# Cosine attention followed by a gated feed-forward on one core: the last batch's layout and stores, one kv copy, two x chunks placed anew, six x buffers

## The chip, the cores and the metric

The kernel runs on one core of a Trainium2 chip. Its time is in device microseconds, from start to end of one execution; a profile of one execution gives a span that is about 1.8 us shorter. Engines are called PE (matrix engine; PEld is its weight load), DVE (VectorE), ACT (ScalarE), POOL (GpSimd) and SP (SyncE). A DMA transfer lands when the trace shows its completion; a stop is a stretch in which PE has nothing to do. A run counts as slow when it lies over 1.5% above the fastest of its kernel.

Ratios are the mean time of one kernel's fast runs over that of the kernel before in the same rounds, so not quite the ratio of the medians quoted beside them. Stops of PE are worked out from start times as in the prediction.

## The reference

Shortened; what is left out is reshaping and types.

```python
def _attn_ref(q, k, v):                     # (8, 8, 576, 64): batch, head, position, dim
    theta = pi / 2 * arange(S) / S          # cos, sin of it: one weight per position
    phi = lambda x: concat([relu(x) * cos, relu(x) * sin], -1)
    kv  = einsum('bhsf,bhsd->bhfd', phi(k), v);  z = sum(phi(k), axis=2)
    num = einsum('bhsf,bhfd->bhsd', phi(q), kv)
    den = einsum('bhsf,bhf->bhs', phi(q), z)[..., None] + 1e-06
    return num / den

def reference(...):
    x = attn_out.transpose(0, 2, 1, 3).reshape(4608, 512)
    return ((x @ w1) * (x @ w2) @ w3) @ w_out        # 512 -> 1024 -> 1024 -> 512
```

## The kernel before

Tokens go through the feed-forward in nine tiles of 512. The attention of batch t+1 is woven between the matmuls of tile t: each tile has 24 slots, and a schedule hangs small pieces of attention into them. A batch of 576 positions is five chunks (four of 128 rows, one of 64). Per chunk: features of k, q and v; kv accumulated over the chunks; num (the product with q's features); division into a block xblk; transposition of that block into xT, the operand of the feed-forward. For batches 0 and 1 PE transposes and an engine copies the result; from batch 2 on a DMA transposes.

```python
        if i == NCH - 1:                                    # kv of batches 1 to 7 complete
            kvs = sm.tile([P, H, D + 1], BF16, name="kvs", bufs=2)
            nc.scalar.copy(out=kvs[:, 0:4, :], in_=kvt[:, 0, 0:260])
            nc.vector.tensor_copy(out=kvs[:, 4:8, :], in_=kvt[:, 1, 0:260])
...
        xblk = sm.tile([P, 2, 4, D], BF16, name="xblk", bufs=4)      # in num(b, c)
        def normalize():
            den = sm.tile([P, 2, 4], FP32, name="den")
            nc.vector.tensor_scalar_add(out=den[rows], in0=n4[:, :, :, 64], scalar1=1e-6)
            nc.vector.reciprocal(out=den[rows], in_=den[rows])
            nc.vector.tensor_tensor(out=xblk[rows], in0=n4[:, :, :, 0:D], in1=..., op=ALU.mult)
...
        if b >= 2:                                                   # in x_tr(b, c)
            nc.sync.dma_start_transpose(out=xT[t][:, :, ds(o, R)], in_=xf)
            return
...
        for kc in range(4):
            nc.tensor.transpose(pst[:, kc, 0:R], xf[:, ts(kc, 128)], identb[rows, rows])
        copy = nc.vector.tensor_copy if by_vector else nc.scalar.copy
        copy(out=xT[t][:, :, ds(o, R)], in_=pst[:, 0:4, 0:R])
...
        for i, rows in enumerate(parts):                    # store: two halves of 64 partitions
            on = eng[i % 2] if isinstance(eng, tuple) else eng
            on.dma_start(out=rows[:, :, cols], in_=osb[64 * i:64 * i + rows.shape[0], :, cols])
...
        if t == NT - 1:                                     # the last 128 rows of the output
            for half in range(2):
                cols, n = ts(half, 256), 256
                ops = ffn_tile()
                ...                                         # eight matmuls of n columns
                nc.vector.tensor_copy(out=osb[:, 1, cols], in_=ops[:, 0:n])
                store((nc.sync, nc.scalar), osb[:, 1:2, :], 4 * t + 3, 1, cols)
```

In batches 1 to 7 positions are laid on partitions as 64 x 5 and 64 x 4, so an output tile of 128 partitions falls into two separate blocks of rows, and each store into two halves. Batch 0 alone is laid out as 128 x 4 rows plus 64.

Of the kernel before, what the change touches and what calls it, by code (L numbers as in the profile page):

```python
# [16 lines left out]
P = 128  # L17
H, S, D = 8, 576, 64
F = 2 * D
NCH = 5  # L20
# [48 lines left out]
def kernel(  # L69
# [34 lines left out]



    raw = {}

    def load(b, which, part=None):
        for name in which:  # L110
            src = {"k": k, "v": v, "q": q}[name]
            if part != 1:
                raw[b, name] = ld.tile([P, H, NCH, D], BF16, name=name + "s")
                nc.gpsimd.dma_start(
                    out=raw[b, name][0:64, :, :, :].rearrange("p h j d -> p h (j d)"),
                    in_=src[b, :, 0:320, :].rearrange("h (p j) d -> p h (j d)", j=5))
            if part != 0:
                nc.gpsimd.dma_start(
                    out=raw[b, name][64:128, :, 0:4, :].rearrange("p h j d -> p h (j d)"),
                    in_=src[b, :, 320:S, :].rearrange("h (p j) d -> p h (j d)", j=4))  # L120

    def load_first(eng, t, src, c0=0, n=4):
        rows = src[0, :, 0:512, :].rearrange("h (p j) d -> p h j d", j=4)
        eng.dma_start(out=t[:, :, c0:c0 + n, :].rearrange("p h j d -> p h (j d)"),  # L124
                      in_=rows[:, :, c0:c0 + n, :].rearrange("p h j d -> p h (j d)"))

    def load_first4(eng, t, src):
        eng.dma_start(out=t[0:64, :, 4, :], in_=src[0, :, 512:S, :].rearrange("h p d -> p h d"))

    woutb = wst.tile([P, 8, DM], BF16, name="woutb", bufs=1)  # L130
    w3b = wst.tile([P, 8, DFF], BF16, name="w3b", bufs=1)
# [118 lines left out]
    def features(b, dst, src, c, cos=True, sin=True, scalar_heads=H):  # L250

        R = ROWS[c]
        at = c if b == 0 else NCH + c
        if cos:
            nc.vector.tensor_scalar(out=dst[:R, c, :, 0:D], in0=src[:R, :, c, :], scalar1=0.0,  # L255
                                    scalar2=cosv[:R, at:at + 1], op0=ALU.max, op1=ALU.mult)
        if sin:
            n = scalar_heads
            nc.scalar.activation(out=dst[:R, c, 0:n, D:F], in_=src[:R, 0:n, c, :], func=ACTF.Relu,  # L259
                                 scale=sinv[:R, at:at + 1], bias=0.0)  # L260
            if n < H:
                nc.vector.tensor_scalar(out=dst[:R, c, n:H, D:F], in0=src[:R, n:H, c, :],
                                        scalar1=0.0, scalar2=sinv[:R, at:at + 1],
                                        op0=ALU.max, op1=ALU.mult)
# [16 lines left out]
    def kv_chunk(b, c, i):  # L281
        kp, qp, va = feat[b]
        if i == 0:
            att_of(b)["kv"] = ps_att.tile([P, 2, 512], FP32, name="pnum")
        kvt = att[b]["kv"]
        for h in range(H):
            nc.tensor.matmul(kvt[:, h // 4, ds((h % 4) * 65, 65)], lhsT=kp[:, c, h, :],  # L287
                             rhs=va[:, c, h, 0:D + 1], start=(i == 0 and h % 4 == 0),
                             stop=(i == NCH - 1 and h % 4 == 3))
        if i == NCH - 1:  # L290
            kvs = sm.tile([P, H, D + 1], BF16, name="kvs", bufs=2)
            nc.scalar.copy(out=kvs[:, 0:4, :], in_=kvt[:, 0, 0:260])
            nc.vector.tensor_copy(out=kvs[:, 4:8, :], in_=kvt[:, 1, 0:260])  # L293
            att[b]["kvs"] = kvs

    def kv_first():
# [38 lines left out]
    def num(b, c, chain=True):  # L335
        rows = out_rows(b, c)
        R = ROWS[c]
        at = columns_of(b, c) - rows.start
        qpT, kvs = att[b]["qpT"], att[b]["kvs"]
        if b == 0 and c == 0:  # L340
            nt = ps_first.tile([P, 2, 512], FP32, name="pfirst")
        else:
            nt = ps_att.tile([P, 2, 512], FP32, name="pnum")
        for h in range(H):
            nc.tensor.matmul(nt[:, h // 4, ds((h % 4) * 65, 65)], lhsT=qpT[:, h, ds(at, 128)],  # L345
                             rhs=kvs[:, h, :], start=True, stop=True)
        n4 = nt[rows, :, 0:260].rearrange("p g (h e) -> p g h e", e=65)
        xblk = sm.tile([P, 2, 4, D], BF16, name="xblk", bufs=4)
        att[b]["x"][c] = xblk

        def normalize():
# [3 lines that stand above are left out]
            nc.vector.tensor_tensor(out=xblk[rows], in0=n4[:, :, :, 0:D],  # L355
                                    in1=den[rows].unsqueeze(3).to_broadcast([R, 2, 4, D]),
                                    op=ALU.mult)

        if chain:
            normalize()  # L360
        return normalize
# [24 lines left out]
    def attention_at(b, slots, kv, tr, nu, xt):  # L386

        each = list(enumerate(order_of(b)))
        for i, c in each:
            slots[kv[i]].append(lambda c=c, i=i: kv_chunk(b, c, i))  # L390
            if c not in dma_q(b):
                slots[tr[i]].append(lambda c=c: q_tr(b, c))
        for i, c in each:
            if xt[i] > nu[i]:
                slots[xt[i]].append(lambda c=c: x_tr(b, c))
        for i, c in each:
            slots[nu[i]].append(lambda c=c: num(b, c))
            if xt[i] == nu[i]:
                slots[xt[i]].append(lambda c=c: x_tr(b, c))


    def rows_of(b, c, n):

        if b == 0:
            if c == 4:
                return [out[512:S, :].rearrange("(p j) m -> p j m", j=1)]
            return [out[0:512, :].rearrange("(p j) m -> p j m", j=4)[:, c:c + n, :]]
        lower = out[ds(b * S, 320), :].rearrange("(p j) m -> p j m", j=5)
        upper = out[ds(b * S + 320, 256), :].rearrange("(p j) m -> p j m", j=4)
        return [h[:, c:c + n, :] for h in ((lower,) if c == 4 else (lower, upper))]  # L410

    def store(eng, osb, g, n, cols=slice(0, DM)):

        pair, r = divmod(g, 9)
        b, c = (2 * pair, r) if r < 4 else (2 * pair + 1, r - 5)
        if r == 4:
            parts = rows_of(2 * pair, 4, 1) + rows_of(2 * pair + 1, 4, 1)
        elif n == 1 or c + n <= 4:
            parts = rows_of(b, c, n)
        else:  # L420
            parts = None
        if parts is None or (r == 4 and n > 1):
            for i in range(n):
                store(eng, osb[:, i:i + 1, :], g + i, 1, cols)
            return
        for i, rows in enumerate(parts):
            on = eng[i % 2] if isinstance(eng, tuple) else eng
            on.dma_start(out=rows[:, :, cols], in_=osb[64 * i:64 * i + rows.shape[0], :, cols])  # L428

    ffn_tiles = [0]  # L430

# [16 lines left out]
    def ffn_groups(t):  # L448
# [8 lines left out]
        def on_half(half):  # L457

            for pair in range(2):
                a, b = ffn_tile(), ffn_tile()  # L460
                if pair == 0:
                    for quarter in range(2):
                        for i in range(2):
                            for ps, w in ((a, w1b), (b, w2b)):
                                products(ps[:, ds(256 * i + 128 * quarter, 128)], w, i,
                                         ds(256 * half + 128 * quarter, 128))
                            if half == 0 and quarter == 0 and i == 0:
                                yield
                        if quarter == 0:
                            yield  # L470
                else:
                    for ps, w in ((a, w1b), (b, w2b)):
# [24 lines left out]
        for ms in range(3 if t == NT - 1 else 4):  # L497
# [6 lines left out]
            if ms % 2 == 0:  # L504
                if 1 <= t <= 4:
                    osb = held_pool[0].tile([P, 2, 512], FP32, name="held")
                else:
                    osb = fsb.tile([P, 2, 512], FP32, name="osb", bufs=2)
            nc.scalar.copy(out=osb[:, ms % 2, :], in_=ops[:, :])  # L509
            if t == NT - 1:  # L510
                store((nc.sync, nc.scalar), osb[:, ms % 2:ms % 2 + 1, :], 4 * t + ms, 1)
            elif ms % 2 == 1 and 1 <= t <= 4:
                held.append((osb, 4 * t + ms - 1))
            elif ms % 2 == 1:
                store(nc.gpsimd, osb[:, :, :], 4 * t + ms - 1, 2)
            yield
        if t == NT - 1:
            for half in range(2):
                cols, n = ts(half, 256), 256
                ops = ffn_tile()  # L520
                for jc in range(8):
                    nc.tensor.matmul(ops[:, 0:n], lhsT=abT[:, jc, ts(3, 128)],  # L522
                                     rhs=w34b[:, jc, cols], start=(jc == 0), stop=(jc == 7))
                nc.vector.tensor_copy(out=osb[:, 1, cols], in_=ops[:, 0:n])
                store((nc.sync, nc.scalar), osb[:, 1:2, :], 4 * t + 3, 1, cols)
            yield


# [58 lines left out]
    for t in range(NT):  # L587
        slots = [[] for _ in range(24)]
        if t == 0:
            slots[1].append(lambda: x_tr(0, 1, by_vector=True))  # L590
            slots[1].append(lambda: q_tr(0, 3, evac=False)[1]())
            slots[1].append(lambda: num(0, 2))
            slots[3].append(lambda: x_tr(0, 2))
            slots[3].append(lambda: num(0, 3))
            slots[4].append(lambda: x_tr(0, 3))
            slots[6].append(lambda: prep_q(0, 4))
            slots[11].append(lambda: feature_buffers(1))
            slots[8].append(lambda: q_tr(0, 4))
# [72 lines left out]
```

## Time and profile before

| | kernel before |
|---|---|
| median of 3 runs | 252.97 us (252.49 to 253.37) |
| the profiled run | 253.31 us, span 251.5 us, clock 1.0 |
| PE / DVE / ACT / POOL busy | 97% / 55% / 50% / 36% |
| DMA engines' busy slices, first 100 us | nearly all 9 tenths |
| landing of an x transpose after its issue | 2.3 us at least, 5.0 median, 8.6 at most |

PE is the bound; what counts is where it stands still. The views that show this are in the prediction.

### The profile page before, as it was taken

To read this page: it belongs to the slowest core of one execution; us is meant where nothing else is said; L and a number is where in the kernel's file an instruction comes from. 1 tells how busy PE (TensorE), PEld (TensorE's weight loads), DVE (VectorE), ACT (ScalarE), POOL (GpSimd) and SP (SyncE) were. 2 spreads that over 40 slices of the span, in tenths; PEclk is the share of its full clock that TensorE was granted. 3 is DMA by queue.
4 is the path that set the end of the run, shared out by engine and by line. 5 is a ranking of instruction groups with operands and counts; after the bars stand their busy time and mean duration, and the time that the engine had idled before them with its cause. 6 is when DMAs were issued, how large, how long until landed. Compare 5 with 4: busy or idle time off the path is not lost.

```text
span 251.5 us, 4960 instructions
## 1 busy us (share of the span) xinstructions
PE 243.8 (97%) x1871; PEld 129.9 (52%) x1871; DVE 137.2 (55%) x336; ACT 126.8 (50%) x217; POOL 90.4 (36%) x171
## 2 busy tenths in 40 slices
PE   8899999999999999999999999999999999999993
PEld 2578555666555455545544554555455444444442
DVE  7675665747789628904971594279128504303321
ACT  2676316925976656565655665565532242323320
POOL 7764155540524612441442327270464040022000
PEclk9999999999999999999999999999999999999999
DMA  7999999999989999999899999997699842014014
GB/s 197 180 194 199 210 204 204 198 199 198 254 112 176 182 184 139 213 152 154 127 135 153 179 127 138 242 236 151 120 275 272 113 122 59 3 39 128 0 46 126
DMA packets 79161, 39.86 MB, mean 159 GB/s; under 512 B 46752, under 2 KB 75680, under 8 KB 79136
## 3 DMA queue, kind: packets, MB, share of 16 engines
q0 software_dynamic: 35488, 27.20, 67.5%
q1 hardware_dynamic: 43248, 11.80, 34.4%
q10 hardware_dynamic: 400, 0.52, 0.6%
q8 instruction: 15, 0.25, 0.4%
q14 instruction: 10, 0.08, 0.1%
HBM read 38.80 MB, written 9.44 MB: 192 GB/s over the span
## 4 chain that ended last, share of the span: by engine, by line
PE 86%; DMA 7%; DVE 2%; ACT 2%; issue 1%; POOL 1%; POOLq 0%; DVEq 0%
PE ffnps L454 47%; PE ffnps L500 22%; PE ffnps L222 5%; PE pnum L345 3%; PE pnum L287 3%; DMA xT<-xblk 3%; DMA qs<-in_q_dram 3%; PE pst L318 2%; PE pst L210 1%; PE pst L382 1%; ACT kp L259 1%; PE ffnps L522 1%; DVE xblk L355 1%; POOL vs L124 0%; DVE abT L495 0%
## 5 line engine op out<-in xcount | busy, mean ns | idle before, releaser
L495 DVE TENSOR_TENSOR abT<-asb,ffnps 128x512 bf16<-128x512 bf16 x68 | 46.3, 681 | 71.3 <-PE ffnps L454 69.9
L454 PE MATMUL ffnps<-xT,w1b 128*128 128x512 bf16 (+2 forms) x320 | 74.9, 357 | 0.3 <-DVE xT L384 0.2
L454 PE MATMUL ffnps<-xT,w2b 128*128 128x512 bf16 (+2 forms) x320 | 74.9, 357 | 0.0
L491 ACT CAST asb<-ffnps 128x512 bf16<-128x512 f32 x68 | 39.8, 586 | 59.9 <-PE ffnps L454 50.1
L500 PE MATMUL ffnps<-w34b,abT 128*128 128x512 bf16 x280 | 63.2, 379 | 0.6 <-DVE abT L495 0.6
L454 PEld LDWEIGHTS <-w1b 128*128 128x128 bf16 x320 | 29.4, 98 | 29.5 <-issue 0.7
L500 PEld LDWEIGHTS <-abT 128*128 128x128 bf16 x280 | 26.8, 98 | 32.0 <-DVE abT L495 1.0
L454 PEld LDWEIGHTS <-w2b 128*128 128x128 bf16 x320 | 26.8, 98 | 20.3
L259 ACT ACTIVATE qp<-qs,sinv 128x512 bf16<-128x512 bf16 (+2 forms) x40 | 28.3, 718 | 1.7 <-DMA qs<-in_q_dram 1.6
L428 POOL DMA_DIRECT2D out_dram<-osb x20 | 10.6, 535 | 51.0 <-ACT osb L509 51.0
L355 DVE TENSOR_TENSOR xblk<-pnum,den 128x512 bf16<-128x512 f32 (+1 forms) x39 | 26.9, 690 | 2.5 <-DMA xT<-xblk 1.1
L279 POOL COPY va<-vs 128x512 bf16<-128x512 bf16 (+1 forms) x30 | 18.5, 625 | 22.9 <-DMA vs<-in_v_dram 22.9
L259 ACT ACTIVATE kp<-ks,sinv 128x512 bf16<-128x512 bf16 (+1 forms) x35 | 24.9, 723 | 0.0
L509 ACT COPY osb<-ffnps 128x512 f32<-128x512 f32 x19 | 11.1, 586 | 22.7 <-PE ffnps L500 22.7
L345 PEld LDWEIGHTS <-qpT 128*128 128x128 bf16 x320 | 15.1, 98 | 8.8 <-issue 0.8
L345 PE MATMUL pnum<-kvs,qpT 128*128 128x65 bf16 x312 | 16.5, 194 | 0.3 <-DVE kvs L293 0.3
L287 PEld LDWEIGHTS <-kp 128*128 128x128 bf16 x280 | 13.1, 98 | 7.1
L255 DVE TENSOR_SCALAR qp<-qs,cosv 128x512 bf16<-128x512 bf16 (+1 forms) x40 | 16.4, 416 | 0.5 <-DMA qs<-in_q_dram 0.5
L509 ACT COPY held<-ffnps 128x512 f32<-128x512 f32 x16 | 9.4, 586 | 14.3 <-PE ffnps L500 14.3
L222 PE MATMUL ffnps<-woutb,w3T 128*128 128x512 bf16 x64 | 15.4, 379 | 0.0
L535 POOL COPY seen<-kp 128x1 bf16<-128x1 bf16 (+1 forms) x20 | 3.8, 188 | 29.2 <-DVE kp L255 20.5
L287 PE MATMUL pnum<-va,kp 128*128 128x65 bf16 x280 | 14.1, 193 | 0.0
(87 smaller groups left out, 194.6 us busy)
## 6 DMA issues: line engine op xcount, KB each, us to landing
out_dram<-held POOLq DMA_DIRECT2D x10, 256.0 KB, 4.7
qs<-in_q_dram POOLq DMA_DIRECT2D x9, 256.0 KB, 8.1
ks<-in_k_dram POOLq DMA_DIRECT2D x7, 320.0 KB, 10.3
qs<-in_q_dram POOLq DMA_DIRECT2D x7, 320.0 KB, 7.4
vs<-in_v_dram POOLq DMA_DIRECT2D x7, 320.0 KB, 8.7
w3b<-in_moe_w_dram POOLq DMA_DIRECT2D x8, 256.0 KB, 12.7
ks<-in_k_dram POOLq DMA_DIRECT2D x7, 256.0 KB, 5.6
vs<-in_v_dram POOLq DMA_DIRECT2D x7, 256.0 KB, 9.8
```

Source lines behind the costliest of these rows:

```text
L222: nc.tensor.matmul(acc[:, :], lhsT=w3T[:, lc, :], rhs=woutb[:, lc, :], start=(lc == 0), stop=(lc == 7))
L255: nc.vector.tensor_scalar(out=dst[:R, c, :, 0:D], in0=src[:R, :, c, :], scalar1=0.0, scalar2=cosv[:R, at:at + 1], op0=ALU.max, op1=ALU.mult)
L259: nc.scalar.activation(out=dst[:R, c, 0:n, D:F], in_=src[:R, 0:n, c, :], func=ACTF.Relu, scale=sinv[:R, at:at + 1], bias=0.0)
L279: eng.tensor_copy(out=feat_of(b)[2][:R, c, :, 0:D], in_=raw[b, "v"][:R, :, c, :])
L287: nc.tensor.matmul(kvt[:, h // 4, ds((h % 4) * 65, 65)], lhsT=kp[:, c, h, :], rhs=va[:, c, h, 0:D + 1], start=(i == 0 and h % 4 == 0), sto ...
L345: nc.tensor.matmul(nt[:, h // 4, ds((h % 4) * 65, 65)], lhsT=qpT[:, h, ds(at, 128)], rhs=kvs[:, h, :], start=True, stop=True)
L355: nc.vector.tensor_tensor(out=xblk[rows], in0=n4[:, :, :, 0:D], in1=den[rows].unsqueeze(3).to_broadcast([R, 2, 4, D]), op=ALU.mult)
L454: nc.tensor.matmul(out, lhsT=w[:, kc, ts(jc, 128)], rhs=x[:, kc, tok], start=(kc == 0), stop=(kc == 3))
L491: nc.scalar.copy(out=asb[:], in_=aT[:, :])
L495: nc.vector.tensor_mul(out=abT[:, jc, :], in0=asb[:], in1=bT[:, :])
L500: nc.tensor.matmul(ops[:, :], lhsT=abT[:, jc, ts(ms, 128)], rhs=w34b[:, jc, :], start=(jc == 0), stop=(jc == 7))
L509: nc.scalar.copy(out=osb[:, ms % 2, :], in_=ops[:, :])
```

## The change

Its intent: close the short stops of PE, and shorten the end. The last batch gets batch 0's layout so that the last tile is stored in whole tiles of 128 partitions; kv is copied by one instruction; in the first tile the fourth num comes ahead of the third chunk's transposes, and the fourth chunk's transposes move behind the first matmuls of the second half; batch 1's fourth chunk is copied by VectorE; the last 128 rows of the output are finished in pieces of 256, 128 and 128 columns in place of two of 256, each stored by one queue; there are six x buffers, and one output buffer moves to another pool to make room.

```diff
+    own = (0, B - 1)                       # batches laid out as 128 x 4 rows + 64
...                                         (loads, tables and output rows follow `own`)
-            nc.scalar.copy(out=kvs[:, 0:4, :], in_=kvt[:, 0, 0:260])
-            nc.vector.tensor_copy(out=kvs[:, 4:8, :], in_=kvt[:, 1, 0:260])
+            nc.vector.tensor_copy(out=kvs[:].rearrange("p (g h) e -> p g (h e)", g=2),
+                                  in_=kvt[:, :, 0:260])
...
-        xblk = sm.tile([P, 2, 4, D], BF16, name="xblk", bufs=4)
+        xblk = sm.tile([P, 2, 4, D], BF16, name="xblk", bufs=6)
...
-                slots[xt[i]].append(lambda c=c: x_tr(b, c))
+                slots[xt[i]].append(lambda c=c, i=i: x_tr(b, c, by_vector=(i == 3)))
...
-                            if half == 0 and quarter == 0 and i == 0:
+                            if quarter == 0 and i == 0:
                                 yield
-                        if quarter == 0:
+                        if half == 0 and quarter == 0:
                             yield
...
-                    osb = fsb.tile([P, 2, 512], FP32, name="osb", bufs=2)
+                    pool = (fsb, held_pool[0])[ms // 2]
+                    osb = pool.tile([P, 2, 512], FP32, name="osb", bufs=1)
...
-                store((nc.sync, nc.scalar), osb[:, ms % 2:ms % 2 + 1, :], 4 * t + ms, 1)
+                store((nc.sync, nc.scalar)[ms % 2], osb[:, ms % 2:ms % 2 + 1, :], 4 * t + ms, 1)
...
-            for half in range(2):
-                cols, n = ts(half, 256), 256
+            for at, n, eng in ((0, 256, nc.scalar), (256, 128, nc.sync), (384, 128, nc.scalar)):
+                cols = ds(at, n)
...
-                store((nc.sync, nc.scalar), osb[:, 1:2, :], 4 * t + 3, 1, cols)
+                store(eng, osb[:, 1:2, :], 4 * t + 3, 1, cols)
...
-            slots[3].append(lambda: x_tr(0, 2))
             slots[3].append(lambda: num(0, 3))
-            slots[4].append(lambda: x_tr(0, 3))
+            slots[3].append(lambda: x_tr(0, 2))
+            slots[5].append(lambda: x_tr(0, 3))
```

More of the change, by code (lines that the diff above doesn't have):

```diff
@@ L102, with load_first, load_first4 @@
     ctx.enter_context(tc.manual_schedule())
+    own = (0, B - 1)
     raw = {}
+    def load_first(eng, t, src, c0=0, n=4, b=0):
+        rows = src[b, :, 0:512, :].rearrange("h (p j) d -> p h j d", j=4)
+        eng.dma_start(out=t[:, :, c0:c0 + n, :].rearrange("p h j d -> p h (j d)"),
+                      in_=rows[:, :, c0:c0 + n, :].rearrange("p h j d -> p h (j d)"))
+    def load_first4(eng, t, src, b=0):
+        eng.dma_start(out=t[0:64, :, 4, :], in_=src[b, :, 512:S, :].rearrange("h p d -> p h d"))
     def load(b, which, part=None):
@@ L113, in load @@
                 raw[b, name] = ld.tile([P, H, NCH, D], BF16, name=name + "s")
+            if b in own:
+                if part != 1:
+                    load_first(nc.gpsimd, raw[b, name], src, b=b)
+                if part != 0:
+                    load_first4(nc.gpsimd, raw[b, name], src, b=b)
+                continue
+            if part != 1:
                 nc.gpsimd.dma_start(
@@ L120, in load @@
                     in_=src[b, :, 320:S, :].rearrange("h (p j) d -> p h (j d)", j=4))
-    def load_first(eng, t, src, c0=0, n=4):
-        rows = src[0, :, 0:512, :].rearrange("h (p j) d -> p h j d", j=4)
-        eng.dma_start(out=t[:, :, c0:c0 + n, :].rearrange("p h j d -> p h (j d)"),
-                      in_=rows[:, :, c0:c0 + n, :].rearrange("p h j d -> p h (j d)"))
-    def load_first4(eng, t, src):
-        eng.dma_start(out=t[0:64, :, 4, :], in_=src[0, :, 512:S, :].rearrange("h p d -> p h d"))
     woutb = wst.tile([P, 8, DM], BF16, name="woutb", bufs=1)
@@ L252, in features @@
         R = ROWS[c]
-        at = c if b == 0 else NCH + c
+        at = c if b in own else NCH + c
         if cos:
@@ L402, in rows_of @@
     def rows_of(b, c, n):
-        if b == 0:
+        if b in own:
             if c == 4:
-                return [out[512:S, :].rearrange("(p j) m -> p j m", j=1)]
-            return [out[0:512, :].rearrange("(p j) m -> p j m", j=4)[:, c:c + n, :]]
+                return [out[b * S + 512:(b + 1) * S, :].rearrange("(p j) m -> p j m", j=1)]
+            rows = out[b * S:b * S + 512, :].rearrange("(p j) m -> p j m", j=4)
+            return [rows[:, c:c + n, :]]
         lower = out[ds(b * S, 320), :].rearrange("(p j) m -> p j m", j=5)
@@ L426, in store @@
         for i, rows in enumerate(parts):
-            on = eng[i % 2] if isinstance(eng, tuple) else eng
-            on.dma_start(out=rows[:, :, cols], in_=osb[64 * i:64 * i + rows.shape[0], :, cols])
+            eng.dma_start(out=rows[:, :, cols], in_=osb[64 * i:64 * i + rows.shape[0], :, cols])
     ffn_tiles = [0]
@@ L592 @@
             slots[1].append(lambda: num(0, 2))
+            slots[3].append(lambda: num(0, 3))
             slots[3].append(lambda: x_tr(0, 2))
-            slots[3].append(lambda: num(0, 3))
-            slots[4].append(lambda: x_tr(0, 3))
+            slots[5].append(lambda: x_tr(0, 3))
             slots[6].append(lambda: prep_q(0, 4))
```

## The prediction

> **What bounds the kernel now.** I read the page first (busy shares, slices), then who the matrix engine waited for, then the timeline around each wait, and last the landing times of loads, transposes and stores.
>
> ```profile
> PE 243.8 (97%) x1871; PEld 129.9 (52%) x1871; DVE 137.2 (55%) x336; ACT 126.8 (50%) x217; POOL 90.4 (36%) x171
> ...
> PE   8899999999999999999999999999999999999993
> ```
>
> The matrix engine (PE) is busy everywhere at 251.5 us of span except in the first two slices and the last, at a granted clock of 1.0, and no other engine passes 55%. So only three things can shorten this kernel: less PE work, fewer PE gaps, or shorter ends. The change leaves PE's work alone (eight 256-column matmuls become sixteen 128-column ones at the very end), so I priced the gaps. The waits of PE alone:
>
> ```profile
> PE ffnps L500 <- DVE abT L495: 0.6, 1, 0.6
> PE pst L382 <- DVE xblk L355: 0.3, 1, 0.3
> PE pnum L345 <- DVE kvs L293: 0.3, 1, 0.3
> PE ffnps L454 <- DVE xT L384: 0.2, 1, 0.2
> ```
>
> This view understates them, since a matmul's end is modelled and overlaps its successor. I measure a gap by pitch: eight 512-column matmuls in a row take 1.73 us in the chain, 0.216 each; a 256-column one takes 0.11 (16 in 1.76), a 128-column one 0.055 (four start every 0.22). A gap is the next start minus (start + count x pitch). After 17 us exactly four gaps exceed 0.12 us.
>
> Gap 1, first token tile. PE would be free at 20.18 + 8 x 0.108 = 21.04; it restarts at 21.56: 0.52 us, waiting for the fourth x chunk's division.
> ```profile
> 20.18 1.04 PE L454 MATMUL ffnps<-xT,w2b 128*128 128x256 bf16 x8
> ...
> 21.56 0.40 PE L382 MATMUL pst<-identb,xblk 128*128 128x128 bf16 x4 [0.35 <-DVE xblk L355]
> ```
> The same stretch shows the num of that chunk at 19.92, its xblk on VectorE from 20.82, and ScalarE's copy of the transposes from 22.00 to 22.59.
>
> Gap 2, kv of batch 1. PE free at 52.82 + 4 x 0.216 = 53.68, restart 54.14: 0.46 us. ScalarE's half goes first and VectorE's waits for it, back to back.
> ```profile
> 52.82 1.02 PE L500 MATMUL ffnps<-w34b,abT 128*128 128x512 bf16 x4
> 53.24 0.38 ACT L292 CAST kvs<-pnum 128x260 bf16<-128x260 f32 x1
> ...
> 53.66 0.43 DVE L293 CAST kvs<-pnum 128x260 bf16<-128x260 f32 x1 [2.92 <-ACT kvs L292]
> 54.14 0.42 PE L345 MATMUL pnum<-kvs,qpT 128*128 128x65 bf16 x8 [0.30 <-DVE kvs L293]
> ```
> Gap 3, start of tile 1. PE free at 63.04 + 0.86 = 63.90, restart 64.22: 0.32 us. The copy of tile 1's last x chunk stands in ScalarE's queue behind a feature activation (62.96, 0.73 us).
> ```profile
> 63.04 1.02 PE L500 MATMUL ffnps<-w34b,abT 128*128 128x512 bf16 x4
> ...
> 63.58 0.58 ACT L384 COPY xT<-pst 128x512 bf16<-128x512 bf16 x1
> ...
> 64.22 1.02 PE L454 MATMUL ffnps<-xT,w1b 128*128 128x512 bf16 x4
> ```
> Gap 4, last batch. PE free at 198.12 + 7 x 0.216 = 199.63, restart 200.35: 0.72 us. The fifth xblk had to wait for a buffer (four exist): the first DMA transpose, issued at 190.65, took 8.26 us to land. VectorE runs in order, so the product abT behind it was late too.
> ```profile
> 198.12 1.67 PE L500 MATMUL ffnps<-w34b,abT 128*128 128x512 bf16 x7
> 199.01 0.69 DVE L355 TENSOR_TENSOR xblk<-pnum,den 128x512 bf16<-128x512 f32 x1 [1.15 <-DMA xT<-xblk]
> 199.62 0.68 DVE L495 TENSOR_TENSOR abT<-asb,ffnps 128x512 bf16<-128x512 bf16 x1
> ...
> 200.35 5.57 PE L500 MATMUL ffnps<-w34b,abT 128*128 128x512 bf16 x25 [0.56 <-DVE abT L495]
> ```
> The four sum to 2.02 us, 0.8% of the time: the ceiling for everything before the tail.
>
> **What the Trainium skill says.** "Perfetto Trace Analysis", section Optimization Strategy: find the gaps on the engine that limits, and what releases each; that is the method above. "VectorE: DVE Perf Modes", section The TRN2 errata: a PSUM-to-SBUF instruction costs 120 cycles plus its elements at 0.96 GHz, so 396 ns for 260 and 667 ns for 520 elements. The trace has 429 ns for 260, 8% more; I therefore estimate 0.43 + 260/960 = 0.70 us for the merged copy. "DMA: Bandwidth & Descriptors", section Rules for kernel authors: two transfers to disjoint partition halves share the same engines, so one transfer of 128 partitions is as good; and its section Anatomy of one DMA gives about 2.0 us of fixed cost, mostly completion. The trace agrees: the last stores of 64 KB land 1.93 (SyncE) and 2.47 us (ScalarE) after issue, those of 128 KB 2.35 to 3.13.
>
> **The change part by part.**
> 1. First tile. The fourth num moves ahead of the third chunk's transposes, so it starts 0.23 us sooner (19.69). Its xblk then starts at about 20.59 (VectorE is still busy with abT to 20.15) and ends at 21.28. The fourth chunk's transposes now follow eight matmuls of half 1, so PE issues them at 21.04 + 8 x 0.055 = 21.48 without waiting: the old gap disappears. But the ScalarE copy follows the transposes by 0.44 us as now (21.56 to 22.00), at 21.92, and ends at 22.51; PE has work until 21.48 + 0.22 + 0.44 = 22.14, then stops about 0.4 us for this chunk. The second quarter starts at 22.55 instead of 22.69 (as read off the matmuls now). Gain 0.15, not 0.52.
> 2. kv in one piece. VectorE is idle at that point (2.92 us of wait), so the copy starts when the kv matmuls are done, about 53.05, and ends at 53.75. PE restarts near 53.79 instead of 54.14. Gain 0.35. For batches 2 to 7 a gap of work lies between kv and num already: nothing gained; VectorE gets 7 x 0.27 = 1.9 us more work, ScalarE 7 x 0.38 = 2.7 less, neither near its limit.
> 3. Tile 1's last chunk on VectorE. It comes after the three kp features that end at 62.95, takes 0.43, ready near 63.40; needed at 63.90. The gap closes. Gain 0.31.
> 4. Six xblk buffers. The fifth xblk runs straight after its reciprocal, 197.90 to 198.59; abT ends near 199.25, needed at 199.63. Gain 0.72. The moved osb buffer only makes room for this.
> 5. Last batch's layout. The last tile's stores are one of 128 rows in place of two of 64; inside the run nothing waits for them. At the end the last copy is of 128 columns: 0.42 - 128/960 = 0.29 us, 0.13 sooner; sixteen 128-column matmuls cost 16 x 0.055 - 8 x 0.108 = 0.02 more. The last store is again 64 KB on ScalarE's queue. Gain 0.1. The loads change too: per tensor 512 rows of 640 B (86 ns a packet between 146 and 164 us) and 512 of 512 B (60 ns), 4.7 us of the 16 DMA engines, become 1024 of 512 B and 512 of 128 B (32 ns in the first 12 us), about 5.0. That is 0.3 us more per tensor, far from any use.
>
> Sum: 0.15 + 0.35 + 0.31 + 0.72 + 0.1 = 1.63 us. 252.97 - 1.63 = 251.3.
>
> **The rivals.**
> - Gap 1 only changes its releaser. I already book most of it as lost; should ScalarE's asb copy be in the way of the chunk, nothing is left: 251.5. If the chunk is no limit, all 0.52 comes: 251.0.
> - PE, arriving 0.8 us sooner, runs into the loads of the first 70 us, where the DMA slices read 9. For: the va copies for batch 2 end at 66.7 and kv uses them at 67.0. Against: these copies follow a GpSimd store that waits for a ScalarE copy which moves forward with PE; w3 lands 1.3 us before its use. Worth up to 0.5 lost: 251.8.
> - The finer loads of the last batch slow the transposes for tile 5: the second one landed at 155.6, used at 158.5. With 0.3 us more per tensor, the 2.9 us should hold; if not, a new gap of up to 1 us: 252.3.
> - The tail gets longer: 128 short rows of 512 B on one queue in place of 64 of 1 KB on each of two. For: stores from ScalarE land 0.3 to 0.5 us later than SyncE's of the same moment. Worth 0.3 either way.
>
> **Range and chances.** The three runs before lie within 0.35% (252.49 to 253.37), about 0.4 us either side of the median, which is of the size of my uncertain terms. All gaps closed and a shorter tail give 250.6; two rivals together give 252.4. Hence 250.3 to 252.4 for 8 in 10. Faster by over 2% means under 247.9, more than all gaps together: 1%. Slower by over 2% needs a new 5 us wait that nothing here prepares: 1%. Within 2%: 98%.
>
> **What would show it.** In the changed kernel: no VectorE wait for a transpose ahead of xblk; PE's wait before the first num of batch 1 under 0.15 us; no wait at the start of tile 1; the first tile's gap smaller and released by ScalarE's xT copy; a kvs copy of about 0.70 us; the last copy about 0.29 us and its store landing about 2.5 us later. I am wrong if a new PE gap over 0.5 us stands anywhere between 64 and 240 us, or if the time from the last matmul to the end grows.

## The result, and the profile after

| | before | after |
|---|---|---|
| median | 253.0 us (252.49 to 253.37, 4 runs) | 251.68 us (251.29 to 252.15, 4 runs) |
| ratio of fast runs | | 0.995 (0.9926 to 0.9974) |
| span of the profiled run | 251.5 us | 249.5 us |

The time fell by 1.3 us, half a per cent, within the predicted range and 0.3 us short of the predicted fall (0.4 by the ratio). The two profiled runs differ by 1.92 us, more than the medians do.

What PE alone waited for in the changed kernel (total us, times, longest):

```profile
PE unread L180 <- DVE zeros L156: 1.2, 1, 1.2
PE kva L312 <- DVE va L287: 0.9, 1, 0.9
PE ffnps L462 <- ACT xT L392: 0.2, 1, 0.2
...
```

Of the five lines of this view four are the start-up before 17 us (two of them shown). The waits for abT, for xblk, and for kvs are gone, and one is new: xT from ScalarE. In time order, from the timeline of the changed kernel:

```profile
21.92 0.59 ACT L392 COPY xT<-pst 128x512 bf16<-128x512 bf16 x1 [0.47 <-PE pst L390]
21.94 0.39 PE L462 MATMUL ffnps<-xT,w2b 128*128 128x128 bf16 x4
...
22.55 0.38 PE L462 MATMUL ffnps<-xT,w1b 128*128 128x128 bf16 x4 [0.23 <-ACT xT L392]
...
52.88 0.70 DVE L300 CAST kvs<-pnum 128x520 bf16<-128x520 f32 x1 [2.13 <-PE pnum L295]
...
53.63 0.42 PE L353 MATMUL pnum<-kvs,qpT 128*128 128x65 bf16 x8
...
62.55 0.42 DVE L392 COPY xT<-pst 128x512 bf16<-128x512 bf16 x1
...
62.61 1.02 PE L508 MATMUL ffnps<-w34b,abT 128*128 128x512 bf16 x4
...
63.47 1.03 PE L462 MATMUL ffnps<-xT,w1b 128*128 128x512 bf16 x4
```

The first tile: PE is through at 21.94 + 4 x 0.055 = 22.16 and goes on at 22.55, a stop of 0.39 us in place of 0.52. kv: the single copy of 0.70 us ends at 53.58 and PE goes on 0.05 us later; the stop is 0.09 us in place of 0.46. Tile 1: 62.61 + 0.86 = 63.47, no stop. The stop near 199 us:

```profile
196.92 0.20 DVE L362 RECIPROCAL den<-den 128x8 f32<-128x8 f32 x1
197.15 0.69 DVE L363 TENSOR_TENSOR xblk<-pnum,den 128x512 bf16<-128x512 f32 x1
...
197.38 1.89 PE L508 MATMUL ffnps<-w34b,abT 128*128 128x512 bf16 x8
197.76 0.68 DVE L503 TENSOR_TENSOR abT<-asb,ffnps 128x512 bf16<-128x512 bf16 x1
```

The fifth block follows its reciprocal at once, abT is done at 198.44 and the eighth matmul, which reads it, could start at 197.38 + 7 x 0.216 = 198.89: no stop.

The end. Four lines of the issue table for the stores of the last pieces (size, median us from issue to landing); the first two are of the kernel before, the next fence is of the changed one:

```profile
out_dram<-osb SPq DMA_DIRECT2D x2, 64.0 KB, 2.1
out_dram<-osb ACTq DMA_DIRECT2D x2, 64.0 KB, 2.5
```

```profile
out_dram<-osb SPq DMA_DIRECT2D x1, 64.0 KB, 2.1
out_dram<-osb ACTq DMA_DIRECT2D x1, 64.0 KB, 1.9
```

The last store of the changed kernel, on ScalarE's queue, lands 1.95 us after issue; that of the kernel before took 2.47. The ends, step by step, from the traces (us from the span's start):

| | last matmul starts | last copy ends | last store issued | landed | end of span | last matmul to end |
|---|---|---|---|---|---|---|
| before | 247.11 | 247.84 | 247.87 | 250.34 | 251.45 | 4.35 |
| after | 245.71 | 246.25 | 246.29 | 248.24 | 249.53 | 3.82 |

So the difference of 1.92 us between the two profiles is 1.40 ahead of the last matmul's start and 0.53 behind it. None of it is the start-up: PE starts the same transposes at 16.99 and 16.98 us. The stops give 0.13 (first tile) + 0.37 (kv) + 0.31 (tile 1) + 0.72 (near 199 us) = 1.53; 0.07 is given back near 57 us, where a stop between transposes and a num grew from 0.11 to 0.18 (in every profile with six buffers, and in none with three, four or five; why is open); the remaining 0.06 is the shorter last matmul, whose start lies nearer to its end.

### The profile page after: what moved, and what is told of

The parts are those of the page before. It is cut to its first block, busy times and chain, and to the rows that moved or that the text cites. A ratio compares the mean times of both kernels' runs of the same rounds, so it can differ in the third digit from the quotient of the medians.

```text
span 249.5 us, 4973 instructions
## 1 busy us (share of the span) xinstructions
PE 242.9 (97%) x1879; PEld 130.2 (52%) x1879; DVE 141.6 (57%) x338; ACT 124.5 (50%) x209; POOL 90.9 (36%) x171
## 4 chain that ended last, share of the span: by engine, by line
PE 92%; DMA 3%; DVE 1%; issue 1%; POOL 1%; ACT 0%; POOLq 0%
PE ffnps L462 50%; PE ffnps L508 24%; PE ffnps L230 6%; PE pnum L353 4%; PE pnum L295 4%; DMA qs<-in_q_dram 3%; PE pst L326 2%; PE pst L218 1%; PE pst L390 1%; PE ffnps L531 1%; POOL vs L112 0%; DVE xblk L363 0%; PE pfirst L353 0%; ACT xT L392 0%; DVE qp L263 0%
```

## The experiments

All twelve gave correct results. They were run in three groups, each on one chip together with its own runs of the kernel before: 252.79 us median in the first group, 252.69 in the second, 252.92 in the third (two of its eleven runs are slow; 252.74 without them). My theory at the start was the prediction's sum, with the end worth more than I had booked. The rivals: the layout of the last batch carries the whole gain; or luck.

Stops of PE in the profile of every run, in us, at the five places that matter (the one at 88 us, the start of tile 2, was not on my list):

| run | first tile | kv, 53 us | tile 1, 64 us | tile 2, 88 us | 199 us |
|---|---|---|---|---|---|
| before | 0.52 | 0.46 | 0.31 | 0 | 0.72 |
| after | 0.39 | 0.09 | 0 | 0 | 0 |
| c_after | 0.39 | 0.09 | 0 | 0 | 0 |
| p_gaps | 0.39 | 0.09 | 0 | 0.14 | 0 |
| t_halves, t_cols | 0.39 | 0.09 | 0 | 0 | 0 |
| p_bufs5 | 0.52 | 0.46 | 0.31 | 0 | 0 |
| p_kv | 0.52 | 0.09 | 0.31 | 0 | 0 |
| p_xvec | 0.52 | 0.46 | 0 | 0 | 0 |
| p_first | 0.39 | 0.46 | 0.31 | 0 | 0 |
| b_look | 0.52 | 0.46 | 0.31 | 0.50 | 0 |
| u_bufs4 | 0.39 | 0.09 | 0 | 1.38 | 0 |
| u_bufs3 | 0.39 | 0.09 | 0 | 0 | 2.97, and three elsewhere |
| g_slot4 | 0.30 | 0.09 | 0 | 0 | 0 |

(In the profiles of the second and third groups some 30 of PE's 1,871 or 1,879 matmul records are missing, scattered; they look like stops of exactly one pitch, 0.216 us, and are left out.)

### First group: the yardstick, the stops alone, and the end (five rounds)

**c_after**: the changed kernel again.

> The changed kernel again, as the yardstick of this group. My theory (four gaps of the matrix engine closed or shortened, 1.45 us in the trace, and an end shorter by 0.47 us) expects 251.1 to 251.7 us, ratio 0.993 to 0.995, and a trace like the first one: one gap of about 0.39 us near 22 us, 0.09 us ahead of the first num of batch 1, no others after 17 us. A rival (the gain is mostly run-to-run luck of the start-up) expects a ratio above 0.997.

Measured: 251.27 us (251.02 to 252.14, 6 runs), ratio 0.9945 (0.9924 to 0.9967). As expected; luck of the start-up is out, since the whole interval lies below that rival's 0.997.

**p_gaps**: the kernel before with everything but the last batch's layout, loads and stores.

```diff
 (kernel before, plus: kv in one copy; by_vector=(i == 3); the new order of the first tile;)
+        xblk = sm.tile([P, 2, 4, D], BF16, name="xblk", bufs=6)
+                    pool = (fsb, held_pool[0])[ms // 2]
+                    osb = pool.tile([P, 2, 512], FP32, name="osb", bufs=1)
```

> The kernel before with the four gap repairs (new order in the first tile, kv in one copy, last chunk of tile 1 on VectorE, six x buffers with the moved output buffer), but the old layout, loads and stores of the last batch. My theory: the last matmul starts 1.4 to 1.5 us sooner than in the kernel before, the time from it to the end stays 4.35 us, so 251.5 us (ratio 0.994), 0.3 to 0.5 us above the changed kernel. Rival (the last batch's layout carries the gain): 252.5 us or more, ratio above 0.998.

Measured: 251.74 us (251.52 to 253.48, 6 runs), ratio 0.997 (0.9943 to 0.9997), last matmul to end 4.30 us. The layout does not carry the whole gain: in the profile the last matmul starts at 245.65 us against 247.11, with the old end behind it. The timing is less sure. Its ratio gives 0.76 us where the four stops should give 1.5, but the interval, which the single run of 253.48 widens, reaches from 0.1 to 1.4 us, and the medians differ by 1.05. I took this as a first hint that one of the four stops is not in every run; it doesn't show it.

**t_halves**: the changed kernel with each store of the last tile cut into two halves of 64 partitions again.

```diff
+            if isinstance(eng, tuple):
+                for j in range(2):
+                    eng[j].dma_start(out=rows[64 * j:64 * j + 64, :, cols],
+                                     in_=osb[64 * j:64 * j + 64, :, cols])
+                continue
...                                         (both stores of the last tile get (nc.sync, nc.scalar))
```

> The changed kernel, with each store of the last tile cut again into two halves of 64 partitions, one on SyncE's and one on ScalarE's queue at the same moment. Theory P (two stores issued at the same moment hold each other up): the later of the last pair lands 2.3 us or more after its issue instead of 1.95, and the time from the last matmul's start to the end goes from 3.8 back to 4.2 to 4.35. Theory H (halves of 64 partitions are slow in themselves): the same. Theory S (it was the smaller last copy and fewer bytes in flight): stays at 3.8 to 3.9, landing near 2.0. Time 0.3 to 0.5 us above the changed kernel under P and H, equal under S.

Measured: 252.22 us (251.81 to 252.89, 6 runs), ratio 0.9979 (0.9958 to 1.0001); last matmul to end 4.56 us, more than P or H asked for. Theory S falls.

**t_cols**: two whole-row stores at the same moment.

```diff
-            for at, n, eng in ((0, 256, nc.scalar), (256, 128, nc.sync), (384, 128, nc.scalar)):
+            for at, n, eng in ((0, 256, nc.scalar), (256, 256, None)):
...
+                if eng is None:
+                    store(nc.sync, osb[:, 1:2, :], 4 * t + 3, 1, ds(256, 128))
+                    store(nc.scalar, osb[:, 1:2, :], 4 * t + 3, 1, ds(384, 128))
```

> The changed kernel with its last 256 columns copied in one piece and then stored as two whole-row stores of 128 partitions by 128 columns, issued at the same moment on the two queues. Parts P from H: under P the later one lands 2.3 us or more after its issue and the end takes about 4.2 us from the last matmul; under H both land about 2.0 to 2.15 us after issue, as single stores do, and the end is longer than the changed kernel's by the longer copy alone (0.13 us), about 3.95.

Measured: 251.67 us (251.55 to 252.05, 6 runs), ratio 0.9962 (0.9941 to 0.9984). The two stores, issued at the same moment, landed after 1.93 and 2.09 us, so P falls for whole rows. H fits these landings, but not as it is worded: SyncE's half in the kernel before landed after 1.93 us too, so a half isn't slow in itself. In the seven profiles with the old stores SyncE's half of the last pair landed after 1.93 to 2.64 us (under 2.1 in five), ScalarE's after 2.42 to 2.62. A single half on ScalarE's queue was not tried, so whether the pairing or the queue makes ScalarE's half late is open. The end took 4.21 us, not 3.95, so H's figure for the whole end was missed. The lines for the output buffer show what differs. Each gives min/median/max of the issuing instruction in ns, the kernel before first:

```profile
L428 SPq DMA_DIRECT2D out_dram<-osb x5: 466/467/546, 242.8 to 247.9; - x5
L428 ACTq DMA_DIRECT2D out_dram<-osb x5: 497/523/672, 242.8 to 247.9; - x5
```

t_halves:

```profile
L438 SPq DMA_DIRECT2D out_dram<-osb x6: 466/503/546, 241.0 to 246.4; - x6
L438 ACTq DMA_DIRECT2D out_dram<-osb x6: 498/556/666, 241.0 to 246.7; - x6
```

t_cols:

```profile
L436 SPq DMA_DIRECT2D out_dram<-osb x3: 332/332/358, 241.3 to 246.3; - x3
L436 ACTq DMA_DIRECT2D out_dram<-osb x3: 338/367/375, 243.0 to 246.3; - x3
```

In these lines issuing a store of 64 partitions costs 466 to 672 ns, one of 128 partitions 332 to 375, whatever the bytes (32 to 256 KB among these). The ends side by side:

| | last copy ends | last issue | issue to landing | landing to end | last matmul to end |
|---|---|---|---|---|---|
| before | 247.84 | 247.87 | 2.47 | 1.11 | 4.35 |
| p_gaps | 246.38 | 246.42 | 2.43 | 1.10 | 4.30 |
| t_halves | 245.92 | 246.68 | 2.29 | 0.98 | 4.56 |
| t_cols | 246.30 | 246.34 | 2.09 | 1.35 | 4.21 |
| c_after | 246.23 | 246.27 | 1.95 | 1.28 | 3.81 |

In t_halves the store had to wait 0.76 us for its queue, which was still issuing the piece before. With whole rows the landing of the last store is 0.2 to 0.5 us quicker. The part from landing to the end varies by 0.37 us and gives some of it back; what decides it is open. Why a 64-partition store costs more to issue is open too: the runs show that it does.

### Second group: one part alone (three rounds)

**p_bufs5**: five buffers. Without the moved output buffer it doesn't fit: a pool asks for 38 KB per partition where 37.75 are left.

```diff
-        xblk = sm.tile([P, 2, 4, D], BF16, name="xblk", bufs=4)
+        xblk = sm.tile([P, 2, 4, D], BF16, name="xblk", bufs=5)
...
-                    osb = fsb.tile([P, 2, 512], FP32, name="osb", bufs=2)
+                    pool = (fsb, held_pool[0])[ms // 2]
+                    osb = pool.tile([P, 2, 512], FP32, name="osb", bufs=1)
```

> The kernel before with five x buffers in place of four and the second output buffer moved to the other pool (without that move it does not fit). Theory (only the last batch's fifth block lacked a buffer): the 0.72 us gap near 199 us is gone, the fifth block follows its reciprocal at once, the other three gaps stay at 0.52, 0.46 and 0.32, so the last matmul starts 0.7 us sooner; 252.1 to 252.4 us. Rival (six are needed, or the wait only moves): the gap stays above 0.3.

Measured: 252.81 us (252.54 to 253.0, 4 runs), ratio 1.0009 (0.9987 to 1.0031). No stop near 199 us, as expected, and no gain, a clear miss of 252.1 to 252.4: the interval leaves room for a gain of 0.3 us at most. (This profile's end took 4.67 us from the last matmul, the longest of the seven with the old stores, and gives 0.3 us of its shorter run back; the four times taken together are no lower either.) The next three say why.

**p_kv**, **p_xvec**, **p_first**: kv in one copy; `by_vector=(i == 3)`; the three schedule lines and two `yield` conditions of the first tile. Each is the kernel before plus those lines of the diff above.

> The kernel before with kv copied in one piece by VectorE. Theory: copy of 0.70 us, the gap near 53 us shrinks from 0.46 to 0.09, nothing else changes; last matmul 0.37 us sooner than it would be; time 0.1 to 0.5 us lower, which three rounds may not tell from nothing. Rival (VectorE's longer copy delays its other work): a new gap over 0.15 us between 64 and 190 us. The wait for an x buffer near 199 us should still be there, of a size that follows the landing of the first transpose.

> The kernel before with the fourth x chunk of batch 1 copied by VectorE. Theory: the 0.32 us gap near 64 us disappears, others stay (0.52, 0.46, and the one near 199 us). Rival: VectorE is in the way there and the gap stays above 0.15.

> The kernel before with the new order in the first tile alone. Theory: the gap of 0.52 us ahead of the fourth chunk's transposes is replaced by one of 0.39 behind them, released by ScalarE's copy; everything after 23 us 0.14 us sooner; time 0 to 0.3 us lower. Rival (the gap goes for good): 0.5 us sooner after 23 us.

Measured: 252.41 us (251.98 to 253.75, 4 runs), ratio 1.0011 (0.9975 to 1.0048); 252.42 (251.97 to 252.79, 4 runs), 0.9993 (0.997 to 1.0017); 252.46 (252.07 to 252.48, the three fast runs; one slow of 256.04 left aside), 0.9991 (0.9965 to 1.0016). The timing resolves none of them. The profiles do: each part removes exactly its own stop (table above) and nothing else. And all three, with four buffers, have no stop near 199 us, though for p_kv and p_xvec it was expected to stay. VectorE in p_kv:

```profile
196.90 0.20 DVE L354 RECIPROCAL den<-den 128x8 f32<-128x8 f32 x1
197.14 0.69 DVE L355 TENSOR_TENSOR xblk<-pnum,den 128x512 bf16<-128x512 f32 x1
```

The block has its buffer at once: in this run the first transpose, issued at 189.89, landed at 196.01, after 6.11 us. The fifth block is ready for its buffer 7.2 us after that issue (190.65 to 197.86 in the kernel before), and the product abT, which VectorE does next, has some 0.4 us to spare, so PE stands only if the first transpose takes over about 7.5 us (8.26 less the stop of 0.72 that it caused). It took 8.26 in the first profile, 6.11, 6.37 and 6.84 in these three.

### Third group: is the stop near 199 us in every run, and can it be forced?

**b_look**: the kernel before once more, one look.

> The kernel before once more, for a second profile. Of ten profiles so far only the first of the kernel before had a first transpose of the last batch slower than 7.2 us (8.26) and a gap near 199 us; three kernels with four buffers had 6.1 to 6.8 us and none. Theory (that gap depends on the run): first transpose between 4.5 and 7.2 us, fifth block at once, no gap near 199 us, last matmul near 246.4 instead of 247.1, the other three gaps as before. Rival (the kernel before has that gap regularly): 0.5 to 0.9 us of gap there again.

Measured: 252.74 us, a single run, so its state is unknown. The first transpose took 7.10 us, the fifth block followed its reciprocal after 0.04 us, no stop near 199 us: the theory holds, by 0.1 us. The last matmul started at 246.66, not 246.4, for the profile has a stop of 0.50 us at another place, the start of tile 2, where PE waited for a transpose of batch 2.

**u_bufs4**: the changed kernel with four buffers.

```diff
-        xblk = sm.tile([P, 2, 4, D], BF16, name="xblk", bufs=6)
+        xblk = sm.tile([P, 2, 4, D], BF16, name="xblk", bufs=4)
```

> The changed kernel with four x buffers again. If the gap near 199 us depends on the run, this is as fast as the changed kernel, ratio to the kernel before 0.993 to 0.997, median 251.2 to 251.8 us, and the fifth block waits under 0.1 us in the profile. If the buffers carry 0.7 us of the gain as predicted: 251.9 to 252.3 us and a wait of about 1.1 us ahead of the fifth block.

Measured: 251.23 us (250.9 to 252.9, 6 runs), ratio 0.9936 (0.9904 to 0.9968): as fast as the changed kernel. The first transpose took 6.13 us, and the fifth block waited 0.03 us. The profiled run was the slowest of the six, 252.9 against 250.9 to 251.5, and its view of PE shows a reason:

```profile
85.79 2.32 PE L508 MATMUL ffnps<-w34b,abT 128*128 128x512 bf16 x10
89.33 1.04 PE L462 MATMUL ffnps<-xT,w1b 128*128 128x512 bf16 x4 [1.22 <-DMA xT<-xblk]
```

A stop of 1.38 us at tile 2's start (PE through at about 87.95): the third transpose of batch 2 was issued at 79.95 and landed at 89.28, after 9.33 us. The same transpose took 5.3 to 8.4 us in the other profiles. In the kernel before PE wants it at 88.6; with the stops closed, at 87.9.

**u_bufs3**: three buffers, so that the block must wait for a later transpose.

```diff
-        xblk = sm.tile([P, 2, 4, D], BF16, name="xblk", bufs=6)
+        xblk = sm.tile([P, 2, 4, D], BF16, name="xblk", bufs=3)
```

> The changed kernel with three x buffers, so that the last batch's fifth block must wait for the second transpose (landing 199 to 202 us in the traces so far) in place of the first (194 to 196). Theory (buffer held until the transpose has landed, VectorE in order, abT behind it): fifth block at the second transpose's landing, abT 1.3 us after that, a gap of the matrix engine of 2 to 4 us near 199 us, time 253.3 to 255.5. Rival (the wait is harmless to the matrix engine): equal to the changed kernel, 251.2 to 251.8.

Measured: 264.86 us (258.63 to 267.64, 4 runs), only the 258.63 fast; 253.3 to 255.5 was expected, so the time is a miss. The second transpose was issued at 200.18 and landed at 208.64. VectorE and then PE of the profiled run:

```profile
205.14 0.20 DVE L362 RECIPROCAL den<-den 128x8 f32<-128x8 f32 x1
208.74 0.69 DVE L363 TENSOR_TENSOR xblk<-pnum,den 128x512 bf16<-128x512 f32 x1 [3.39 <-DMA xT<-xblk]
209.34 0.68 DVE L503 TENSOR_TENSOR abT<-asb,ffnps 128x512 bf16<-128x512 bf16 x1
```

```profile
205.60 1.67 PE L508 MATMUL ffnps<-w34b,abT 128*128 128x512 bf16 x7
210.08 6.16 PE L508 MATMUL ffnps<-w34b,abT 128*128 128x512 bf16 x20 [2.80 <-DVE abT L503]
```

The mechanism is as I read it from the kernel before, and now large: block, abT, and a stop of PE of 210.08 - (205.60 + 7 x 0.216) = 2.97 us. But I had counted on one such stop; there are four (1.68, 1.53, 3.00, 2.97 us), because with three buffers the same happens in other batches. And the two long ones cost more than their length. The windows view of this run, PE's granted clock after the row's counts:

```profile
150.00:158.00 8.00, 5.98 (x41) 2.77 (x40) 4.59 (x12) 3.09 (x6) 2.80 (x5) 1.00 1.18 149
158.00:163.00 5.00, 4.13 (x12) 1.57 (x13) 1.86 (x6) 1.50 (x3) 3.27 (x7) 0.66 0.94 143
163.00:168.00 5.00, 4.95 (x33) 2.40 (x33) 0.00 (x0) 3.06 (x6) 1.30 (x3) 1.00 1.25 195
```

After the stop that ends at 158.87 the clock is 0.66 in the mean of 5 us: the trace's clock record shows half rate for 3.41 us, and eight matmuls start 0.40 to 0.43 us apart instead of 0.216. The same follows the stop that ends at 210.08. The stops of 1.5 and 1.7 us are followed by no such stretch. As an estimate, stops of 9.2 us in all and two times half of 3.41 us make 12.6 us; this span is 12.9 us longer than the changed kernel's. So the slow state of the profiled run is accounted for by its own stops; the other slow runs were not profiled. The fast run, 258.63, is still 7 us above the fast runs of the same group's four- and six-buffer kernels (one run against twelve).

**g_slot4**: an attempt to beat both kernels.

```diff
-            slots[5].append(lambda: x_tr(0, 3))
+            slots[4].append(lambda: x_tr(0, 3))
```

> The changed kernel with the fourth chunk's transposes one step earlier, ahead of half 1's first eight matmuls. Working from the changed trace: block ready at 21.28, transposes at 21.33 after a gap of about 0.28 us, ScalarE's copy 21.77 to 22.36, sixteen matmuls from 21.55 to 22.43, then no gap; second quarter at 22.43 instead of 22.55, so 0.12 us gained, which the timing can't resolve. Rival: the copy is late again and a second gap stays, nothing gained.

Measured: 251.28 us (250.87 to 251.84, 6 runs), ratio 0.9929 (0.9904 to 0.9954). PE in its first tile:

```profile
20.26 1.04 PE L462 MATMUL ffnps<-xT,w2b 128*128 128x256 bf16 x8
21.43 0.40 PE L390 MATMUL pst<-identb,xblk 128*128 128x128 bf16 x4
```

One stop of 0.30 us ahead of the transposes and none behind them; the second quarter starts 2.29 us after the w2b matmuls at 20.26, against 2.38 in the changed kernel (20.17 to 22.55). Gained 0.09 us, 0.12 expected. The timing does not tell it from the changed kernel, so it is a version that is no worse, not one that is shown to be faster.

## Why the prediction was right, and where not

1. **First tile, gain 0.15 booked.** Right: the old stop became one of 0.39 us behind the transposes, with ScalarE's copy starting at 21.92 and the second quarter at 22.55, both to the hundredth as predicted.
2. **kv, 0.35 booked.** Right: copy 0.70 us, stop 0.46 to 0.09; p_kv alone gives the same.
3. **Tile 1, 0.31 booked.** Right: the stop is gone, in p_xvec alone too.
4. **Six buffers, 0.72 booked.** Right as a mechanism (u_bufs3; in the profile before abT's operands were ready by 198.28, and it ran only behind the block, at 199.62), wrong as a size. The failed step is "Gain 0.72": it takes one execution's 8.26 us for the rule. Of six profiles of kernels with four buffers one has the stop. Over all fourteen profiles that transpose took 4.57 to 8.26 us, and over 7.5 only that once. u_bufs4 is as fast as the changed kernel and p_bufs5 no faster than the one before. A gain that comes in one run of six or so, 0.1 us in the mean, is not ruled out. The warning stood in the profile before: transposes landed after 2.3 to 8.6 us with a median of 5.0, and this one had to take over 7.5 to matter.
5. **The end, 0.1 booked.** Wrong in size: the profiles have 0.53 us from the last matmul's start, 0.47 from its end. I took the 2.47 us of ScalarE's last store over unchanged, with only the 0.13 us of the shorter copy as gain. A whole-row store landed after 1.95 and took 0.34 us to issue in place of 0.52. This repeats: from the last matmul's start to the end it is 3.79 to 3.82 us in the five profiles with the new end, 4.30 to 4.67 in the seven with the old one.
6. **The loads of the last batch, nothing booked.** Right in effect: the second transpose for tile 5, my worry at 155.6 us, landed at 151.2. The cost itself was mis-sized. My sum, 1024 x 60 + 512 x 32 ns over 16 engines, is 4.9 us and not 5.0; and in the changed kernel's trace the packets of 512 B took 75 ns in that stretch, not 60, so a tensor costs some 5.8 us of the engines, 1.2 more than before and not 0.3. No stop came of it.

The two errors in size, 0.72 too much and 0.43 too little, pull in opposite directions; that the total came out near is luck in these two terms. Without the stop near 199 us the terms are 0.13 + 0.37 + 0.31 - 0.07 + 0.53 = 1.27 us (the shorter last matmul's 0.06 would raise the first part and lower the last); with it, 1.92 by the same profiles. Predicted were 1.63; timed were 1.3 in the first runs and 1.4 in c_after. The interval of c_after, 0.8 to 1.9 us, holds the first sum and just reaches the second, so the timing agrees with the smaller one but doesn't prove it; what rules out a steady 0.72 is p_bufs5 and the profiles. p_gaps should give 0.74 with the three steady stops alone; its 0.76 by the ratio and 1.05 by the medians don't settle it either.

Of the rivals, a late transfer as I had feared it at 70 us and at tile 5 shows up at tile 2: PE, arriving 0.74 us sooner, finds batch 2's third transpose late in some runs (0.14 us in p_gaps, 1.38 in u_bufs4), and the kernel before has it as well (0.50 in b_look). How often each kernel meets it, three cases in fourteen profiles can't say; a single slow run such as p_gaps' 253.48 fits it, but was not profiled, so that is argued and not shown.

## What to carry to other kernels

Price a gap from several profiles, or from the spread that one profile gives, before booking it: a gap that ends with an engine's work came back in every run to 0.01 us, while the gap near 199 us, which ends with a DMA's landing, was there in one profile of six. Here the closed stops were worth their length and no more; but two stops of 3 us in u_bufs3 cost the half clock behind them as well. Profiles resolved parts (0.1 to 0.4 us) that three rounds of timing couldn't. At the end of a kernel, look at whether the last store goes out whole or in halves and at what its queue is still issuing, not at its bytes alone.

## What the Trainium skill lacked or had wrong

- "VectorE: DVE Perf Modes", section The TRN2 errata, gives 120 cycles plus elements for PSUM to SBUF. Measured here: 429 ns for 260 elements and 700 ns for 520, so a slope of 1.04 ns an element as stated, but a fixed part of about 158 ns, 152 cycles (429 - 260/0.96); the copies of 128 and 256 columns, 292 and 424 ns, say the same. The section does report a measured fixed term of about 150 cycles, but for copies from SBUF; here copies from PSUM show it.
- "DMA: Bandwidth & Descriptors", section Rules for kernel authors, advises one transfer of 128 partitions in place of two halves because they share the engines. The advice holds, but the page lacks what it is worth at the end of a kernel: 332 to 377 ns to issue against 466 to 672, and a last landing after 1.93 to 2.09 us (whole tiles of 64 KB, six profiles) against 2.29 to 2.62 (ScalarE's half, 32 or 64 KB, eight profiles).
- The same page, section Latency and other measured facts, gives a DMA transpose an effective bandwidth, and no page that I read gives the scatter of its latency beside other traffic: the same instruction of the same kernel landed after 8.26 and 7.10 us in two runs, and batch 2's third transpose after 5.3 to 9.3 us over all profiles.
- "TensorE: Matmul & The Clock Gate", section Part 1, has the half-rate state begin after an idle window of about 3.4 us. In u_bufs3 stops of 3.00 and 2.97 us were enough, with half rate for 3.41 us after each; stops of 1.5 and 1.7 us were not. Whether the page's remark that the window runs freely covers this, these runs don't settle.
